# Slab loads in the forward's plan, B's Wqkv transposed between the passes, early dWo in two parts

## The chip, the cores and the metric

One Trainium2 chip, one core of it. The time is device microseconds of one execution; the kernel before has a median of 2160.57 µs over 3 runs (2158.79 to 2169.59). One more execution was profiled: it took 2162.31 µs, and its span in the profile, from the first to the last instruction, is 2160.6 µs.

## What is computed

A forward pass through four layers (A, B, A, B) and its gradients, in bf16, for S = 2048 tokens, D = 640, H = 32 heads of 20:

```python
def _A_ref(x, wqkv, wo):                       # linear attention
    q, k, v = split_heads(x @ wqkv)
    phi = lambda t: jnp.where(t > 0, t + 1, jnp.exp(t)) + 1e-6
    kv  = einsum("bhsd,bhse->bhde", phi(k), v); z = einsum("bhsd->bhd", phi(k))
    o   = einsum("bhqd,bhde->bhqe", phi(q), kv) / (einsum("bhqd,bhd->bhq", phi(q), z) + 1e-6)
    return merge_heads(o) @ wo
def _B_ref(x, wqkv, wo):                       # causal softmax attention, window of 256
    ...
x = x + _A_ref(_layernorm(x), A_wqkv, A_wo)    # layer 0
x = x + _B_ref(_layernorm(x), B_wqkv, B_wo)    # layer 1
x = x + _A_ref(_layernorm(x), A_wqkv, A_wo)    # layer 2, the same weights
x = x + _B_ref(_layernorm(x), B_wqkv, B_wo)    # layer 3, the same weights
_out, _vjp = jax.vjp(_f, A_x, A_wqkv, A_wo, B_wqkv, B_wo); _grads = _vjp(grad_out)
```

The outputs are the last x and the gradients of x and of the four weights. The gradient of B's output weight, dWo, is the sum over layers 3 and 1 of (attention output, transposed) x (gradient that arrives at the layer). For layer 3 that gradient is grad_out itself, so this half of dWo can be formed as soon as the forward has layer 3's attention outputs.

## The kernel before, in words

The program is one class. `run()` calls `forward()`, then the attention backward of layer 3 (`B_attn_bwd(3)`), a phase of matmuls and layer norms (`bwd_phase(3, 2, 1)`), the attention backward of layer 1, and the last phase (`bwd_phase(1, 0, None)`).

**Forward.** Tokens go in 16 tiles of 128. `a_first(0)` and `a_kv(0)` do layer 0 up to its key-value sums. `ab_pass(0)` runs the rest of layer 0, layer 1 and the first part of layer 2 as one pipeline over the tiles. After it `late_q(2)` gives the queries of layer 2 for the first six tiles as fillers, `a_kv(2)` sums layer 2, and `ab_pass(2, True)` runs the rest of layer 2 and layer 3. In that second pass each tile of layer 3 also has its local gradient: `dO_steps` multiplies grad_out by Wo and stores dO (with two further columns a head) to DRAM as `dOpt`. q, k and v of layer 3 are stored to DRAM as `qkvp`.

What a tile of layer 3 does on the engines: TensorE makes 12 score matmuls for a group of four heads (L794), ScalarE (ACT) takes the exponential in two instructions (L798, L801), GpSimd (POOL) masks the diagonal and the oldest block (L807, L812), TensorE multiplies by the values (L832). The output projection (`out_proj`, Wo_B), the residual addition to x, the store of the finished x (`out_dram`), and the two chunks of dO follow.

**What sets the order.** In the forward every instruction is an `op` of a planner (`Sched`): engine, an assumed cost, keys that it reads and writes. `order()` is a list scheduler: each engine takes the op that can start first by the assumed times, among equals the one that was written first; TensorE may look 19 ops ahead of the first one not yet issued. `emit()` issues everything in that order with the order fixed, so each engine's queue is exactly the plan. The written order within a pass comes from due times in units of tiles (`items`, `spread`). Buffers come from rings: a ring of n hands out its tiles in turn, and a new use waits for all users of the use n before.

DMAs are issued from SP's or ACT's queue. Each is queued behind what its engine waits for. The DMAs share eight semaphore lanes: a DMA that takes a lane waits for the one that had it before.

**The end of the forward.** After the second pass come `bflips`: 15 blocks of 128 x 640 of B's Wqkv are transposed by DMA into the rings `ee` and `pp` and stored to DRAM as `WqTB`, gated by the layer norm of tile 15 in layer 3. Then `early_dWo` (L715 to L730): 10 units (5 row blocks x 2 halves of 320 columns) of 16 matmuls each (L723; 128x128 by 128x320), in a ring of two PSUM buffers `mm`, an ACT copy each (L727), and a store from ACT's queue to `dWoB_part`.

**The attention backward.** It works on 8 groups of four heads. For each group `attn_slabs` loads slabs from DRAM: q, k, v and dO transposed (QTg, KTg, VTg, dOTg), and k, q, dO plain (Ksl, Qsl, dOsl); for group 0 the dO ones in two halves of 8 tiles. For layer 3 group 0's loads are issued on SP after the forward. For each group 15 steps follow: pairs of scores and dP on TensorE (L1583), exponential on ACT (L1602), masks on POOL (L1611, L1614), product on VectorE (L1622), a transpose of the product and the accumulating matmuls. Layer 1's group 0 is loaded ahead, within `bwd_phase(3)`, to a region `slabA`.

Of the kernel before, what the change touches and what calls it, by code (L numbers as in the profile page):

```python
# [10 lines left out]
ACT = mybir.ActivationFunctionType  # L11
# [5 lines left out]
P = 128  # L17
# [183 lines left out]
class Kern:  # L201
# [130 lines left out]
    def forward(self):  # L332
# [5 lines left out]
        with ExitStack() as st:  # L338
# [5 lines left out]
            def ring(name, n, shape, dt=BF, **kw):  # L344
# [13 lines left out]
                hnA=ring("hnA", 1, [P, D]), hnTA=ring("hnTA", 3, [P, DT, P]),  # L358
                hnB=ring("hnB", 1, [P, D]), hnTB=ring("hnTB", 3, [P, DT, P]),
# [4 lines left out]
                rt=ring("rt", 2, [P, H], F32), li=ring("li", 2, [P, H], F32),  # L364
            )
            pk = g = self.g
# [14 lines left out]
            R["res"] = Ring(2, tiles=[over_vv(CW) for _ in range(2)], name="res")  # L381
# [4 lines left out]
            wsb = {k: big.tile([P, DT, n], BF, name=k) for k, n in (("Wqkv_B", QT), ("Wo_A", D))}  # L386
# [282 lines left out]
            def b_qkv(l, tt, hnT, qk, v, qT, kT):  # L669
                qkvp_v = self.tm_view(self.sv[l]["qkvp"])  # L670

                def chunk(ci):
                    def f():
# [13 lines left out]
                        if ci in (1, 3):  # L687
# [4 lines left out]
                                [(b, ci - 1), (b, ci)], [])  # L692
                        if ci == 5:
                            dma("SP", lambda: qkvp_v[:, tt, 2 * DP:3 * DP], lambda: v.t.rearrange("p h d -> p (h d)"),
                                256 * KB, [(v, 4), (v, 5)], [])
# [20 lines left out]
            def early_dWo():  # L716
                for m in range(DT):
                    for ci in range(2):
                        ps, res, c0 = R["mm"].buf(), R["res"].buf(), ci * CW
                        for t0, t1 in ((0, 5), (5, 10), (10, TT - 1), (TT - 1, TT)):  # L720
                            def f(ps=ps, m=m, c0=c0, t0=t0, t1=t1):
                                for tt in range(t0, t1):
                                    nc.tensor.matmul(ps.t[:, 0:CW], lhsT=att_out[3, tt][0].t[:, m * P:(m + 1) * P],  # L723
                                                     rhs=g[:, tt, c0:c0 + CW], start=(tt == 0), stop=(tt == TT - 1))
                            op("PE", pe([CW] * (t1 - t0)), f, [("g", tt) for tt in range(t0, t1)] +
                               [(att_out[3, tt][0], q) for tt in range(t0, t1) for q in (0, 1)], [ps])
                        op("ACT", av(CW), lambda ps=ps, res=res: nc.scalar.copy(res.t, ps.t[:, 0:CW]), [ps], [res])  # L727
                        after_kv(S.ops[-1])
# [1101 lines left out]
```

## Time and profile before

| | |
|---|---|
| median of 3 runs | 2160.57 µs (2158.79 to 2169.59) |
| the profiled execution | 2162.31 µs, span 2160.6 µs |
| mean granted TensorE clock | 0.974 |
| PE busy 93%, DVE 66%, ACT 55%, POOL 41% of the span | |
| pass 0 ends, a_kv(2), pass 2 begins | about 398 to 480 µs |
| last score group of the forward | 722.23 µs |
| early dWo on PE | 731.85 to 753.74 µs |
| first pair of the attention backward, layer 3 | 754.52 µs |
| first pair of the attention backward, layer 1 | 1480.91 µs |

Times in rows are microseconds from the start of the span. A row in order of time gives start, length, engine, line of the kernel, operation, what it writes and reads, and how often; rows that follow one another closely are merged. In brackets stands the idle time of the engine before the row, and what ended it. SPq and ACTq are DMA issues on the queues of SP and ACT. Rows "A <- B: us, times, longest" sum what A waited for B. Matmuls are pipelined: the time from one row's start to the next is what counts, not the sum of lengths. Rows by stretch give for each engine busy time and, in brackets, instructions, then the granted TensorE clock (1 is full), the DMA engines' mean busy share, and GB/s.

### The profile page before, as it was taken

The page shows a single profiled execution, that of the slowest core. Times are in us where ns is not written, and L with a number is a line of the kernel's source. Part 1 is how long each engine was busy: PE and PEld are TensorE (multiplying, and loading weights), DVE is VectorE, ACT ScalarE, POOL GpSimd, SP SyncE. Part 2 cuts the span into 40 slices and gives each one's busy share as a digit, 9 for nine tenths or more (in the row PEclk, how much of TensorE's full clock was granted, in tenths as well). Part 3 has the DMA queues.
Part 4 walks back from the last instruction along what each step waited for, and adds up shares of the span by engine and source line. Part 5 has one row for each costly group of instructions (what it writes and reads, how often), then busy time and mean ns, then how long its engine had stood idle before and what let it go on. Part 6 is the DMA issues. An engine that isn't in the chain of part 4 may idle for free. (4 is left out here: it accounts for less than half of the span.)

```text
span 2160.6 us, 67815 instructions
## 1 busy us (share of the span) xinstructions
PE 2004.4 (93%) x27808; PEld 1383.7 (64%) x27808; DVE 1436.1 (66%) x2942; ACT 1195.3 (55%) x1981; POOL 883.0 (41%) x1850
## 2 busy tenths in 40 slices
PE   6878899879999799999899999998999999999999
PEld 4645666556666567777666667645777766666764
DVE  7667677577776289999734459705999985444751
ACT  4627778627788389989622223314989982220430
POOL 1015566416777356666422213203666652220210
PEclk9989999999999889999999999998999999999999
DMA  7459989469999799998998799936999998989944
GB/s 273 172 151 198 194 192 194 116 191 201 210 210 203 167 164 155 156 161 156 180 187 183 197 201 210 186 95 143 158 161 158 157 179 171 197 184 225 183 112 103
DMA packets 964807, 379.70 MB, mean 176 GB/s; under 512 B 844816, under 2 KB 944784, under 8 KB 964240
## 3 DMA queue, kind: packets, MB, share of 16 engines
q1 hardware_dynamic: 886720, 301.59, 72.7%
q10 hardware_dynamic: 77776, 73.79, 11.1%
q8 instruction: 217, 3.56, 0.7%
q14 instruction: 94, 0.77, 0.1%
HBM read 109.02 MB, written 112.07 MB: 102 GB/s over the span
## 5 line engine op out<-in xcount | busy, mean ns | idle before, releaser
L1622 DVE TENSOR_TENSOR ds_sb<-pair,e_sb 128x768 bf16<-128x768 f32 x480 | 438.0, 951 | 78.7 <-PE pair L1583 71.9
L1602 ACT ACTIVATE e_sb<-pair 128x768 bf16<-128x768 f32 x480 | 391.1, 815 | 92.7 <-PE pair L1583 68.0
L807 POOL TENSOR_SCALAR_AFFINE_SELECT e_sb<-e_sb 128x384 bf16<-128x384 bf16 (+1 forms) x512 | 199.5, 409 | 359.5 <-ACT e_sb L798 333.9
L798 ACT ACTIVATE e_sb<-s_ps 128x1152 bf16<-128x1152 f32 (+2 forms) x256 | 273.9, 1070 | 112.5 <-PE s_ps L794 76.9
L1614 POOL TENSOR_SCALAR_AFFINE_SELECT e_sb<-e_sb 128x256 bf16<-128x256 bf16 x448 | 183.1, 409 | 225.7 <-ACT e_sb L1602 225.6
L1068 PE MATMUL dw_ps<-dqkv,om 128*128 128x480 bf16 x1280 | 268.8, 366 | 0.0
L1068 PEld LDWEIGHTS <-om 128*128 128x128 bf16 x1760 | 170.7, 98 | 152.1 <-DMA om<-o 8.1
L1256 POOL TENSOR_TENSOR gw<-w,gcar 128x640 f32<-128x640 f32 x64 | 89.5, 1399 | 421.7 <-ACT w L1253 417.6
L1611 POOL TENSOR_SCALAR_AFFINE_SELECT e_sb<-e_sb 128x256 bf16<-128x256 bf16 x512 | 207.4, 408 | 102.0 <-ACT e_sb L1602 102.0
L1068 PEld LDWEIGHTS <-dqT 128*128 128x128 bf16 x1920 | 185.7, 98 | 71.8 <-issue 0.4
L1647 PEld LDWEIGHTS <-dsT 128*128 128x128 bf16 x2880 | 146.2, 97 | 94.9 <-issue 88.6
L1638 ACT COPY dsT<-dsT_ps 128x768 bf16<-128x768 bf16 x240 | 191.2, 797 | 9.5 <-PE dsT_ps L1635 6.3
L439 PE MATMUL mm_ps<-Wqkv_B,hnTB 128*128 128x320 bf16 x960 | 169.8, 308 | 9.6 <-DVE gcar L511 5.9
L1647 PE MATMUL dqvk_ps<-Ksl,dsT 128*128 128x32 bf16 x2160 | 170.4, 179 | 7.3 <-DMA dsT<-ds_sb 4.5
L1651 PE MATMUL dqvk_ps<-dOsl,e_sb 128*128 128x32 bf16 x2160 | 165.7, 177 | 0.1
L1651 PE MATMUL dqvk_ps<-Qsl,ds_sb 128*128 128x32 bf16 x2160 | 165.8, 177 | 0.0
L1635 PE MATMUL dsT_ps<-ident,ds_sb 128*128 128x128 bf16 x1848 | 157.9, 223 | 1.5 <-ACT dsT L1638 1.3
L1651 PEld LDWEIGHTS <-e_sb 128*128 128x128 bf16 x2880 | 144.9, 96 | 0.2 <-issue 0.2
L1651 PEld LDWEIGHTS <-ds_sb 128*128 128x128 bf16 x2880 | 145.0, 96 | 0.0
L812 POOL TENSOR_SCALAR_AFFINE_SELECT e_sb<-e_sb 128x512 bf16<-128x512 bf16 x224 | 143.1, 639 | 0.0
L801 ACT ACTIVATE e_sb<-s_ps 128x384 bf16<-128x384 f32 (+2 forms) x256 | 119.7, 468 | 36.3 <-PE s_ps L794 13.6
L1068 PE MATMUL dw_ps<-wq,dqT 128*128 128x320 bf16 x960 | 138.1, 299 | 0.3 <-ACT dqkv L1428 0.3
(209 smaller groups left out, 3900.7 us busy)
## 6 DMA issues: line engine op xcount, KB each, us to landing
qkvp<-qk_slab SPq DMA_DIRECT2D x64, 256.0 KB, 3.5
hn<-hn SPq DMA_DIRECT2D x64, 160.0 KB, 3.1
om<-hn SPq DMA_DIRECT2D x20, 512.0 KB, 5.2
qkvp<-v_slab SPq DMA_DIRECT2D x32, 256.0 KB, 3.8
o<-o SPq DMA_DIRECT2D x48, 160.0 KB, 3.1
om<-o SPq DMA_DIRECT2D x15, 512.0 KB, 4.8
Ksl<-qkvp SPq DMA_DIRECT2D x12, 512.0 KB, 5.2
Qsl<-qkvp SPq DMA_DIRECT2D x12, 512.0 KB, 5.3
```

What stands on the lines that cost most here:

```text
L439: nc.tensor.matmul(ps.t[:, w0:w0 + width], lhsT=lhsT(), rhs=rhs(), start=start, stop=stop)
L798: op("ACT", av(3 * nkt * P), lambda: nc.scalar.activation(e.t[:, 0:3, 0:nkt, :], s3.t[:, :, 0:nkt * P].rearrange("p h (i q) -> p h i q", q=P),
L807: nc.gpsimd.affine_select(out=v, in_=v, compare_op=ALU.is_ge, fill=0.0, base=0, pattern=[[0, h1 - h0], [1, P]], channel_multiplier=-1)
L1068: nc.tensor.matmul(ps.t[:, w0:w0 + width], lhsT=lhsT(), rhs=rhs(), start=start, stop=stop)
L1602: nc.scalar.activation(E[n][:, 2 * p:2 * p + 2], PR[h][:, :, 0:3 * P].rearrange("p i (j q) -> p i j q", q=P), ACT.Exp, scale=self.c_att)
L1611: nc.gpsimd.affine_select(out=e[:, :, j, :], in_=e[:, :, j, :], compare_op=ALU.is_ge, fill=0.0, base=0, pattern=[[0, 2], [-1, P]], channel ...
L1614: nc.gpsimd.affine_select(out=e[:, :, j, :], in_=e[:, :, j, :], compare_op=ALU.is_ge, fill=0.0, base=-1, pattern=[[0, 2], [1, P]], channel ...
L1622: nc.vector.tensor_mul(DS[n][:, hs], PR.pop(h)[:, :, 0:3 * P].rearrange("p i (j q) -> p i j q", q=P), E[n][:, hs])
L1635: nc.tensor.transpose(ps[:, i, j, :], DS[n][:, 2 * p + i, j, :], self.ident)
L1638: (nc.scalar.copy if by == "A" else nc.vector.tensor_copy)(TSB[h], TPS.pop(h))
L1647: nc.tensor.matmul(a[:, 0, hh, :], lhsT=TSB[2 * n + hh // 2][:, hh % 2, j, :], rhs=ld[g]["K"][:, k, cs], start=(i == 0), stop=(i == len(dq ...
L1651: nc.tensor.matmul(a[:, 1 + x, hh, :], lhsT=src[n][:, hh, j, :], rhs=ld[g][rhs][:, q, cs], start=(i == 0), stop=(i == len(dkv) - 1))
```

## The change

- A new tile `slabR` of 7 x 2048 columns lives for the whole program. It holds group 0's slabs of layer 3. During the forward, Wqkv_B, Wo_A and the small rings hnA, hnB, rt, li are cut from it; later the backward of layer 3 uses it for even groups' slabs, that of layer 1 for odd groups', and the phases cut rings and sums from it.
- Group 0's nine slab loads become ops of the forward's plan on SP. They wait for the stores that they read and for all readers of Wqkv_B and Wo_A (the plain dO loads also for the users of the small rings).
- The 15 `bflips` stand between the two passes, gated by layer 1's last layer norm, and go through the rings KT, QT and e.
- Early dWo is in two parts. `dWo_most`: units 0 to 5, tiles 0 to 12, due at 15.0 to 16.25 of the second pass, in three chunks (5, 5, 3); the sum is copied in f32 by DVE into x of tiles that are done. `dWo_rest`, at the end: units 6 to 9 with all 16 tiles (an ACT copy each), then the last three tiles of units 0 to 5, added by DVE to what lies in x. It uses the score ring's five PSUM buffers and waits for the last two scores.
- The stores of x and dO of tiles 14 and 15 are issued on SP instead of ACT.

```diff
-    def forward(self):
+    def forward(self, slabs):
...
+            wsb = {k: over_raw(DT * n).rearrange("p (k n) -> p k n", k=DT) for k, n in (("Wqkv_B", QT), ("Wo_A", D))}
+            for k in ("hnA", "hnB"):
+                R[k] = Ring(1, tiles=[over_raw(D)], name=k)
...
+            TS, NA = 13, 6
+
+            def dWo_mm(ps, u, t0, t1, a):
+                m, c0 = u // 2, u % 2 * CW
...
+            def dWo_most(u):
+                def f():
+                    ps = R["mm"].buf()
+                    for t0 in range(0, TS, 5):
+                        dWo_mm(ps, u, t0, min(t0 + 5, TS), 0)
+                    op("DVE", vp(CW), lambda: nc.vector.tensor_copy(x[:, u, :].bitcast(F32), ps.t[:, 0:CW]), [ps],
+                       [("x", u)])
+                return f
+
+            def dWo_rest():
+                scored = [o for k in ("s3", "s1") for b in R[k].items[-2:] for o in b.ops]
+                order = list(range(NA, 2 * DT)) + list(range(NA))
...
+                    b, ps = res[m], R["s"].buf()
...
+                    for t0 in ([0, 5, 10, TS] if u >= NA else [TS]):
+                        dWo_mm(ps, u, t0, min(t0 + 5, TS) if t0 < TS else TT, 0 if u >= NA else TS).deps.update(scored)
+                    if u >= NA:
+                        op("ACT", av(CW), lambda ps=ps, half=half: nc.scalar.copy(half(), ps.t[:, 0:CW]), [ps], [(b, ci)])
+                    else:
+                        op("DVE", vp(CW), lambda ps=ps, half=half, u=u: nc.vector.tensor_add(
+                            half(), ps.t[:, 0:CW], x[:, u, :].bitcast(F32)), [ps, ("x", u)], [(b, ci)])
...
-                        dma("ACT", lambda: self.tm_view(self.dOp[3])[:, tt, :], lambda: slab.t.rearrange(
-                            "p h d -> p (h d)"), 256 * KB, [(slab, i) for i in range(4)], [])
+                        dma("ACT" if tt < TT - 2 else "SP", lambda: self.tm_view(self.dOp[3])[:, tt, :], lambda: slab.t.rearrange(
+                            "p h d -> p (h d)"), 256 * KB, [(slab, i) for i in range(4)], [("dOp", tt)])
...
             def bflips(i, gate):
-                    b = R[("ee", "ee", "pp")[i % 3]].buf()
+                    kind = ("KT", "QT", "KT", "e", "e")[i % 5]
+                    b = R[kind].buf()
...
-                                dma("ACT", lambda: xout[:, tt, :], lambda: x[:, tt, :], 160 * KB, [("x", tt)], [])
+                                dma("ACT" if tt < TT - 2 else "SP", lambda: xout[:, tt, :], lambda: x[:, tt, :], 160 * KB,
+                                    [("x", tt)], [])
...
+                    spread(items, 15.0, 16.25, [dWo_most(u) for u in range(NA)])
...
             ab_pass(0, False)
+            for i in range(3 * DT):
+                bflips(i, ("rs", 1, TT - 1))()
             for tt in range(EARLY):
                 late_q(2, tt, filler=True)
...
             ab_pass(2, True)
-            for i in range(3 * DT):
-                bflips(i, ("rs", 3, 15))()
-            early_dWo()
+            over = [o for k in ("Wqkv_B", "Wo_A") for o in S.rd.get(k, ())]
+            late = [o for k in ("hnA", "hnB", "rt", "li") for b in R[k].items for o in b.ops]
+            for rows, kind, size, f in slabs:
+                keys = [("dOp", t) for t in rows] or [("qkvp", 3, t, i) for t in range(TT) for i in (1, 3, 5)]
+                op("SP", 60, f, keys, [], dma=(kind, size)).deps.update(over + late if rows and kind == "D" else over)
+            dWo_rest()
...
+        self.raw = self.persist.tile([P, 7 * self.T], BF, name="slabR")
...
+        first, slab0 = {}, Cuts(self.raw)
+        self.forward(self.attn_slabs(3, 0, slab0, first))
```

More of the change, by code (lines that the diff above doesn't have):

```diff
@@ L714, in early_dO @@
                     after_kv(S.ops[-1])
[L716 to L728, printed above, removed]
-                        dma("ACT", lambda m=m, c0=c0: self.dWoB_part[m * P:(m + 1) * P, c0:c0 + CW], lambda res=res: res.t,
-                            2 * P * CW, [res], [])
@@ L1138, in bwd_phase @@
                         ("pkT", 2, [P, DT, P], BF), ("vT", 2, [P, DT, P], BF), ("eq", 2, [P, D], BF), ("ek", 2, [P, D], BF)):
-                    R[name] = ring(name, n, shape, dt)
+                    if name != "ek" or far:
+                        R[name] = ring(name, n, shape, dt)
+                if not far:
+                    R["ek"] = Ring(2, tiles=[cuts.tile([P, D], BF, f"ek{i}") for i in range(2)], name="ek")
             if not wide:
@@ L1703, in B_attn_bwd @@
                        lambda g=g, t=t: evac(g, t), [("A", g, t, hh) for hh in range(4)])
[L1704 to L1708 removed]
+            ld[0] = first
             todo = {}
```

76 lines of the change are left out of this document (42 added, 34 removed).

## Prediction, made before the changed kernel was run

> **What bounds the kernel now.** I read the page's head first, then the busy time by stretches of 5 µs around the end of the forward pass, then the engines' rows in order of time there, then the longest waits.
>
> ```profile
> span 2160.6 us, 67815 instructions
> PE 2004.4 (93%) x27808; PEld 1383.7 (64%) x27808; DVE 1436.1 (66%) x2942; ACT 1195.3 (55%) x1981; POOL 883.0 (41%) x1850
> ```
>
> TensorE (PE) is busy for 93% of the span, so a change gains where PE idles, where its clock is low, or where it works alone while nothing that follows can start. The end of the forward has all three. Rows of the stretches (from:to, length, then PE, weight loads, DVE, ACT, POOL, the granted clock, the DMA share):
>
> ```profile
> 700.00:705.00 5.00, 4.19 (x58) 2.62 (x57) 0.49 (x1) 3.50 (x6) 3.82 (x9) 0.53 0.98 249
> 720.00:725.00 5.00, 2.39 (x60) 1.77 (x59) 0.00 (x0) 3.77 (x6) 3.67 (x9) 0.50 1.09 194
> 398.00:440.00 42.00, 33.57 (x523) 24.42 (x522) 25.29 (x71) 18.97 (x36) 12.46 (x28) 0.96 0.25 84
> ```
>
> PE's own rows there (start, length, what, and in brackets the idle time before):
>
> ```profile
> 696.79 0.35 PE L794 MATMUL s_ps<-QT,KT 32*128 32x128 bf16 x12
> ...
> 702.08 0.51 PE L794 MATMUL s_ps<-QT,KT 32*128 32x128 bf16 x12
> 702.52 2.85 PE L439 MATMUL mm_ps<-Wo_B,oTB 128*128 128x320 bf16 x10
> ...
> 705.37 1.49 PE L439 MATMUL mm_ps<-vv 128*128 128x320 bf16 x5
> 706.80 0.49 PE L794 MATMUL s_ps<-QT,KT 32*128 32x128 bf16 x12
> ...
> 712.27 0.35 PE L794 MATMUL s_ps<-QT,KT 32*128 32x128 bf16 x12
> 712.55 0.32 PE L832 MATMUL pv_ps<-v_slab,e_sb 128*128 128x32 bf16 x6
> 712.71 0.43 PE L439 MATMUL mm_ps<-Wo_B,oTB 128*128 128x320 bf16 x2
> ...
> 720.42 0.51 PE L794 MATMUL s_ps<-QT,KT 32*128 32x128 bf16 x12 [1.30 <-ACT e_sb L798]
> ...
> 722.23 0.51 PE L794 MATMUL s_ps<-QT,KT 32*128 32x128 bf16 x12 [0.87 <-ACT e_sb L798]
> ...
> 731.10 0.84 PE L439 MATMUL mm_ps<-vv 128*128 128x320 bf16 x5
> ...
> 733.61 2.06 PE L723 MATMUL mm_ps<-gcar,Wqkv_A 128*128 128x320 bf16 x14
> ...
> 735.79 2.06 PE L723 MATMUL mm_ps<-gcar,Wqkv_A 128*128 128x320 bf16 x14
> ...
> 753.17 0.57 PE L723 MATMUL mm_ps<-gcar,Wqkv_A 128*128 128x320 bf16 x3
> 754.52 0.35 PE L1583 MATMUL pair<-KTg,QTg 32*128 32x128 bf16 x8 [0.78 <-ACT vv L727]
> ```
>
> The last two tiles' 12 score groups start between 696.79 and 722.23, 11 periods in 25.44 µs. ACT's exponentials set the natural period: 720.42 to 722.23 is 1.81. Eleven of these are 19.9, so 5.5 µs are stalls. After the scores PE ends the last dO chunk at 731.94 (731.10 + 0.84) and then does all of early dWo alone until 753.74: 160 matmuls, 16 per 2.18 µs (733.61 to 735.79), 0.136 each. The two stalls and PE's idle time by what it waited for, and then the slab loads and the first work of the attention backward:
>
> ```profile
> ACT e_sb L798 <- DVE vv L754: 3.2, 1, 3.2
> ACT e_sb L798 <- DMA ee<-in_B_wqkv_dram: 3.2, 1, 3.2
> ```
> ```profile
> PE s_ps L794 <- ACT e_sb L798: 6.0, 5, 2.8
> PE pv_ps L832 <- POOL e_sb L812: 5.5, 6, 1.3
> ```
> ```profile
> 740.94 1.27 SPq L326 DMA_TRANSPOSE QTg<-qkvp  x1
> ```
> ```profile
> 758.27 1.82 DVE L1622 TENSOR_TENSOR ds_sb<-pair,e_sb 128x768 bf16<-128x768 f32 x2 [22.60 <-PE pair L1583]
> ```
>
> So the slab loads begin late, at 740.94, and VectorE's first product, from which the attention's own rhythm runs, comes at 758.27, 3.75 µs after the first pair.
>
> **The change, part by part.**
>
> *Dealing 13 tiles of six units under the scores.* 78 of the 160 dWo matmuls move ahead of the dO's end. By the planned order PE gets, between the score group at 696.79 and the last one, 20 Wo_B and 15 dO matmuls that were there before, 65 of dWo (units 0 to 4), about 100 value products and 11 score groups. At full clock: 100 wide ones x 0.136 = 13.6; scores 0.28 a group (712.27 to 712.55), 3.1; values 0.16 for six (712.55 to 712.71), some 3; one set of transposes, 0.3. Sum 20.4, against 25.44 that pass now. Period by period the work is 0.7, 1.8, 1.8, 1.9, 1.8, 1.1, 2.3, 2.0, 1.9, 1.8 and 3.3; where it is under ACT's 1.81 the period is 1.81, which makes 22.3. The stall on the DMA goes: it is ACT standing at an out_dram store that shares a semaphore lane with a Wqkv flip; the flips are moved away and the store goes to SP. Full clock is not to be had throughout: the row of 700 to 705 has 0.53, and what leads to it is not changed. Ten Wo_B took 2.85 at 702.52 where 10 x 0.136 is 1.4, and about the next 1.2 µs of work doubles as well before the busier PE is fast again; half of some 4 µs, 2.0, is added. (Bounds: 0, and 4 if it lasts to 708 as now.) The last scores then start at 696.79 + 22.3 + 2.0 = 721.1, not 722.23.
>
> After it, to the end of dO, PE has 42 value products, 10 Wo_B, 10 dO and 8 transposes as now, 13 matmuls of unit 5 and 8 + 5 of the whole units in gaps that are waits for POOL, DVE and ACT. It takes 9.7 µs now (722.23 to 731.94), at the 0.50 of 720 to 725; with more work but a warmer clock I take 9.35: 730.45. Left are 61 of dWo (units 6 to 9 less what was in the gaps, and 6 x 3): 61 x 0.136 = 8.3, PE ends at 738.7 instead of 753.74: **-15.0**. The copies to x (six, on DVE) and the six additions lie in time in which DVE idles: 0.49 busy of 5 in the first stretch, none in the second. Without that cover the last addition alone would be on the path, about 0.5.
>
> *Slab loads in the plan.* Seven of the nine need only q, k, v and the first dO tiles, all done by 703; they stand on SP from there, ahead of the last stores. The two second halves of dO follow dO's last store. What that gives is seen where layer 1 starts, with its slabs loaded ahead:
>
> ```profile
> 1480.91 0.35 PE L1583 MATMUL pair<-slabA 32*128 32x128 bf16 x8
> ```
> ```profile
> 1481.92 2.36 ACT L1602 ACTIVATE e_sb<-pair 128x768 bf16<-128x768 f32 x3 [24.36 <-DVE res L1171]
> ```
> ```profile
> 1483.61 2.69 DVE L1622 TENSOR_TENSOR ds_sb<-pair,e_sb 128x768 bf16<-128x768 f32 x3 [2.10 <-POOL e_sb L1611]
> ```
>
> 2.70 from first pair to first product, so 1.05 less than in layer 3. But there is a new wait. The last dWoB_part store on ACT shares a lane with the load of dO's second half, and the first exponential is queued on ACT behind that store. The chain of it, with the store's row now and the landing times:
>
> ```profile
> 735.46 0.34 ACTq L407 DMA_DIRECT2D dOpt<-vv  x1
> ```
> ```profile
> WqTB<-ee SPq DMA_DIRECT2D x10, 160.0 KB, 2.8
> dOpt<-vv ACTq DMA_DIRECT2D x4, 256.0 KB, 3.4
> ...
> Qsl<-qkvp SPq DMA_DIRECT2D x1, 512.0 KB, 5.3
> ...
> ee<-in_B_wqkv_dram SPq DMA_TRANSPOSE x8, 4.3
> ...
> dOTg<-dOpt SPq DMA_TRANSPOSE x2, 3.5
> ```
>
> From the dO's end to the store are 3.5 µs (731.94 to 735.46), its landing 3.4, the load's landing 3.5, the freed store's issue 0.3: 730.45 + 10.7 = 741.2. Without it the exponential would start at 738.7 + 0.8 (the pair's wait for an evacuation, as at 754.52) + 1.0 = 740.5. So the exponential is at 741.2, and the product 1.7 later (1481.92 to 1483.61), at 742.9: **-15.4** against 758.27.
>
> *Flips between the passes.* 15 flips and 15 stores on SP, and their place on it:
>
> ```profile
> 722.34 1.28 SPq L411 DMA_TRANSPOSE pp<-in_B_wqkv_dram  x1
> 723.66 0.58 SPq L407 DMA_DIRECT2D WqTB<-pp  x1
> ```
> ```profile
> 403.53 23.24 SPq L407 DMA_DIRECT2D hn<-hnA  x3
> ```
> ```profile
> 478.26 0.28 PE L439 MATMUL mm_ps<-mbd,pqT 128*128 128x32 bf16 x5
> ```
>
> 15 x (1.28 + 0.58) = 28 µs of SP. SP there issues three hn stores in 23 µs, mostly waiting, and the DMA share of 398 to 440 is 0.25, so the flips fit up to about 437. Behind them stand the pqT flips of later tiles, the third of which PE needs at 478.26. New lane sharing holds single ACT stores for about 1 µs. ACT is busy 18.97 of 42 there. I take **+1.0**, with bounds -1 and +3.
>
> *The rest.* The order of PE from the attention backward on is the old one, so a shift at 758 is carried to the end. The backward phases cut their rings from the new tile; loads wait for the same last readers to within a group, and the memsets of layer 1's sums move a little on DVE: 0, within 1.5 either way. The absence of the 15 flips from the forward's end is counted with the stall; the DMA share of about 1 there makes anything more possible, nothing less.
>
> **Sum**: -15.4 + 1.0 = -14.4. The profiled execution took 2162.31 µs (span 2160.6 and 1.7 around it), so it becomes 2147.9; it was 1.74 above the median of three, 2160.57, and by the same step the median becomes **2146.2**.
>
> **Rivals.**
>
> 1. *The clock stays high* (0.14). With dWo in the waits PE has hardly a gap, so the 0.53 stretch may vanish, and the moved flips cost nothing: 2.0 and 1.0 more gain, and 1 from DMA relief: -17.4 to -18.4, 2142 to 2143. For it: PE's waits in 690 to 760 are 6.0 for ACT and 5.5 for POOL, and those are what is filled. Against it: the drop to 0.53 comes before the first dealt matmul.
> [...]
>
> 2. *The dealt matmuls delay the scores* (0.14). PE takes its queue in order. A chunk of 5 is 0.68 at full clock and 1.36 at half; each ahead of a score group can hold ACT, which is the rhythm. 18 chunks at 0.6 are 10.6 µs, all that was moved. If nothing hides, what stays is the DMA stall (up to 3.2), the 1.05 of the slabs, and 1 to 3 of filled waits after the last scores, less 1.0: -4 to -6, so 2155 to 2157. For it: six periods are over 1.81 even at full clock. Against it: 5.5 µs of stalls and 6.0 of waits for ACT are there to be filled.
>
> 3. *The slabs do not come early* (0.12). The lane chain above is within 0.7 µs of the bound. Each of its landings at 5.3, the Qsl row, instead of 3.4 and 3.5 delays the first exponential by 3.7: 2149.9. So the change would not do in full what its first part says. For it: seven loads and four stores on one SP queue, and a DMA share near 1. Against it: the flips that fill the queues now are gone.
>
> 4. *Slower* (0.06): the flips between the passes run one at a time. Each store waits for its flip, each buffer for its store, behind scores and values that use the same buffers: 15 x (4.3 + 2.8) = 106 µs from 403.53, to 510. The pqT flip behind them would be 32 late at PE's 478.26, less 15.4: +16, 2177. It decides from (478.3 - 403.5 + 15.4) / 15 = 6.0 µs a flip. Against it: eleven buffers are in rotation, not one, and the DMA share there is 0.25, where the present place has about 1.
>
> **How the numbers follow.** The forecast has 0.54, spread over 2143 to 2150. About 0.5% (10.8 µs) is what a measurement of this kernel can tell from no change, which puts the border at 2149.8. Faster: 0.51 of the forecast's, 0.14 of the first rival and 0.06 of the third, 0.71. Same: 0.03, 0.14 and 0.06, 0.23. Slower: 0.06. The range goes from 2140 (first rival, with the memsets' 1.5) to 2156.5 (most of the second), and leaves out the fourth and some of the ends.
>
> **What would show it.** Right: dWo rows between the last score groups; PE's last dWo matmul near 739; the slab loads from about 703; the first product near 743, and the same shift up to the end; no ACT wait of 3 µs for a flip after 710; 398 to 480 longer by no more than 3. Wrong: score periods of 2.5 and more with ACT waiting for PE (second); a first exponential after 743 held by a store (third); a PE wait for pqT between 440 and 480 (fourth); clock 1.0 in 700 to 710 (first). A changed length between 760 and the end would mean that the rings' new places matter, which I cost at nothing.

## The result, and the profile after

| | before | after | ratio after / before |
|---|---|---|---|
| first comparison, median of 22 executions each | 2161.78 µs | 2156.60 µs | 0.9974 [0.9962, 0.9985] |
| a second comparison (35 and 12 executions) | 2165.67 µs | 2157.50 µs | 0.9963 [0.9950, 0.9977] |
| the profiled execution (span) | 2162.31 µs (2160.6) | 2163.08 µs (2161.4) | |

By the ratios the change gains 5.6 µs (0.26% of 2161.78; the two medians differ by 5.2) in the first and 8.0 µs in the second comparison; 14.4 were forecast. The sign was right, the size was not: 2156.60 lies just above the range's upper end, 2156.5. The profiled execution of after happens to be one of its longest, so its span can't be set against that of before; its parts can.

The page's head for after, then three stretches of the forward's end:

```profile
span 2161.4 us, 67833 instructions
PE 2008.5 (93%) x27808; PEld 1384.3 (64%) x27808; DVE 1441.9 (67%) x2954; ACT 1191.9 (55%) x1975; POOL 879.2 (41%) x1850
```
```profile
700.00:705.00 5.00, 4.01 (x67) 2.67 (x66) 3.54 (x8) 3.36 (x5) 4.43 (x8) 1.00 0.27 57
720.00:725.00 5.00, 4.21 (x77) 2.97 (x76) 1.32 (x3) 4.04 (x6) 2.92 (x7) 1.00 1.16 216
702.00:753.00 51.00, 45.59 (x649) 31.88 (x647) 24.68 (x55) 25.25 (x37) 26.66 (x54) 1.00 0.65 150
```

The clock is 1.00 in the two windows in which before had 0.53 and 0.50. As this profile stands 12 µs late here (see below), its 702 to 753 is the work that before does from 690 to 741. The clock is 1.00 over it, against 0.80:

```profile
690.00:741.00 51.00, 38.51 (x552) 26.27 (x551) 18.84 (x44) 25.25 (x36) 27.16 (x55) 0.80 0.78 162
```

PE's rows of after at the forward's end, then ACT's and DVE's first work of the attention backward:

```profile
732.36 0.34 PE L828 MATMUL s_ps<-QT,KT 32*128 32x128 bf16 x12
...
740.63 0.84 PE L446 MATMUL mm_ps<-vv 128*128 128x320 bf16 x5
741.31 0.98 PE L730 MATMUL s_ps<-gcar,Wqkv_A 128*128 128x320 bf16 x6
...
749.87 1.38 PE L730 MATMUL s_ps<-gcar,Wqkv_A 128*128 128x320 bf16 x9 [0.65 <-DVE hnTA L761]
751.18 0.57 PE L1629 MATMUL pair<-slabR 32*128 32x128 bf16 x8
753.73 1.20 PE L1629 MATMUL pair<-slabR 32*128 32x128 bf16 x10 [1.98 <-ACT e_sb L1648]
```
```profile
752.87 1.51 ACT L1648 ACTIVATE e_sb<-pair 128x768 bf16<-128x768 f32 x2 [4.42 <-DMA dWoB_part<-pp]
```
```profile
754.55 2.71 DVE L1668 TENSOR_TENSOR ds_sb<-pair,e_sb 128x768 bf16<-128x768 f32 x3 [2.13 <-PE pair L1629]
```

This profile of after stands 12.1 µs late when the last two tiles' scores begin: the group that started at 696.79 in before starts at 708.90. With 12.1 taken off, the forecast's steps read:

| step | forecast | after, less 12.1 |
|---|---|---|
| last score group | 721.1 | 720.3 |
| end of dO on PE | 730.45 | 729.4 (740.63 + 0.84) |
| end of dWo on PE | 738.7 | 739.1 (749.87 + 1.38) |
| first exponential | 741.2 | 740.8 |
| first product | 742.9 | 742.4 |

The forecast of this stage held to about 1 µs, the first exponential by some luck. As named, it stands on ACT behind the last dWoB_part store. But that store did not wait for its lane. These are SP's dO store and the load of dO's second half, DVE's last additions, and the stores:

```profile
744.98 0.33 SPq L414 DMA_DIRECT2D dOpt<-vv  x1
747.07 1.17 SPq L326 DMA_TRANSPOSE slabR<-dOpt  x1
```
```profile
750.47 1.69 DVE L761 TENSOR_TENSOR pp<-s_ps,x 128x320 bf16<-128x320 f32 x4 [0.66 <-PE s_ps L730]
```
```profile
751.00 1.77 ACTq L414 DMA_DIRECT2D dWoB_part<-pp  x4
```

The dO store landed in 2.0 µs and the load in 3.1, where 3.4 and 3.5 were assumed, so the lane was free at 750.2. The last store went out at 752.4, behind the last addition, which ends at 752.2. The forecast's two paths to the exponential, by the lane and by PE, lay 0.7 apart, so the time came out although the path was the other one.

So 15.5 µs were won here, and 12.1 were missing before it began.

To see where, the start of each PE matmul in before is subtracted from its start in another kernel's profile. A step of this shift is time that one section lost or won. A single profile wanders: the kernel before, profiled once more, was 3.3 late at 420 and 4.5 at 1812 with nothing changed. So each section is read over all profiles:

| kernel | between the passes, 403 to 520 | end of forward, 692 to 763 | 1779 to 1800 | another section | sum | measured, from the ratio |
|---|---|---|---|---|---|---|
| after | +6.4 | -15.5 | +4.0 | | -5.1 | -5.6 |
| after again | +7.2 | -15.6 | +2.6 | | -5.8 | -8.0 |
| before again | +3.3 | -1.1 | +0.9 | | +3.1 | +1.5 |
| flips only | +6.3 | -2.9 | +1.4 | | +4.8 | +0.9 |
| flips after hn | +12.7 | -15.7 | +3.6 | | +0.6 | +2.4 |
| dWo at the end | +6.2 | -5.9 | +3.1 | | +3.4 | +7.8 |
| flips first | -0.4 | -15.7 | +1.8 | +14.0 before 150 | -0.3 | +3.7 |
| memset last | +6.1 | -15.4 | +0.9 | | -8.4 | -7.1 |
| flips first, memset last | -0.5 | -15.8 | +2.5 | +14.2 before 150 | +0.4 | -1.5 |
| flips in pass 2 | +4.2 (to about 480) | -15.8 | +2.7 | +31.1 (480 to 692) | +22.2 | +19.9 |
| flips at the end | +1.6 | -2.7 | +2.8 | | +1.7 | +2.8 |
| slabs in the program | +7.3 | -15.5 | +3.7 | | -4.5 | -7.4 |
| small flips | +7.7 | -15.8 | +2.7 | +13.3 before 113 | +7.9 | +6.3 |

The sum is that of the columns ahead of it, without the drift in the sections that no kernel changes. The last column is (ratio - 1) times the median of before on that chip. Sum and measurement differ by up to 4.4 (dWo at the end), which is how far a single profile can be trusted.

### The profile page after: what moved, and what is told of

The parts are those of the page before. It is cut to its first block, busy times and chain, and to the rows that moved or that the text cites. A ratio compares the mean times of both kernels' runs of the same rounds, so it can differ in the third digit from the quotient of the medians.

```text
span 2161.4 us, 67833 instructions
## 1 busy us (share of the span) xinstructions
PE 2008.5 (93%) x27808; PEld 1384.3 (64%) x27808; DVE 1441.9 (67%) x2954; ACT 1191.9 (55%) x1975; POOL 879.2 (41%) x1850
## 3 DMA queue, kind: packets, MB, share of 16 engines
q10 hardware_dynamic: 77200, 72.94, 10.9%
## 5 line engine op out<-in xcount | busy, mean ns | idle before, releaser
L1113 PEld LDWEIGHTS <-slabR 128*128 128x128 bf16 x1920 | 185.7, 98 | 116.2 <-DMA slabR<-o 5.8
L446 PE MATMUL mm_ps<-slabR,hnTB 128*128 128x320 bf16 x960 | 170.5, 309 | 8.4 <-DVE gcar L518 6.1
L1697 PEld LDWEIGHTS <-e_sb 128*128 128x128 bf16 x2880 | 145.2, 96 | 0.0
L1113 PE MATMUL dw_ps<-dqkv,slabR 128*128 128x480 bf16 x640 | 134.6, 366 | 0.0
L1113 PE MATMUL dw_ps<-dqkv,om 128*128 128x480 bf16 x640 | 134.2, 366 | 0.0
L1284 ACT ACTIVATE dh<-mm_ps 128x320 f32<-128x320 f32 x64 | 28.0, 437 | 191.6 <-PE mm_ps L1113 153.3
L1629 PE MATMUL pair<-slabR 32*128 32x384 bf16 (+2 forms) x1024 | 121.6, 329 | 11.5 <-DVE ds_sb L1668 5.0
L866 PE MATMUL pv_ps<-v_slab,e_sb 128*128 128x32 bf16 x2880 | 117.7, 177 | 12.9 <-POOL e_sb L846 10.7
L866 PEld LDWEIGHTS <-e_sb 128*128 128x128 bf16 x2880 | 106.0, 96 | 35.6 <-POOL e_sb L846 14.6
```

What stands on the lines that cost most here:

```text
L446: nc.tensor.matmul(ps.t[:, w0:w0 + width], lhsT=lhsT(), rhs=rhs(), start=start, stop=stop)
L866: nc.tensor.matmul(pv.t[:, h % 16, :], lhsT=e.t[:, hh, j, :], rhs=vts[j].t[:, h, :], start=(j == 0), stop=(j == nkt - 1))
L1113: nc.tensor.matmul(ps.t[:, w0:w0 + width], lhsT=lhsT(), rhs=rhs(), start=start, stop=stop)
L1697: nc.tensor.matmul(a[:, 1 + x, hh, :], lhsT=src[n][:, hh, j, :], rhs=ld[g][rhs][:, q, cs], start=(i == 0), stop=(i == len(dkv) - 1))
```

## The experiments

Each was timed in five rounds (flips small in three) against the kernel before on the same chip.

**The kernel before, once more.** No edit. Expected:

> The kernel before with nothing changed, as a second look at it. In the two profiles at hand the changed kernel is 6 us late already at 440 us, in a part of the forward that the change does not reorder. If that is chance between two executions, this profile differs from the first one of the kernel before by several us there too (up to 6), and its time ratio is 1.000 within 0.1%. Rival: cutting the small rings and two weights from the new tile costs 6 us early in the forward; then this profile agrees with the first one within 1 us at 440, and every kernel with the new tile is some 6 late there.

Measured: 1.0007 [0.9991, 1.0022]. So intervals of this width can tell 0.2 to 0.3%, and the +5.4 that after's first profile shows at 300 µs, where nothing was changed, is most likely chance: before again is at +3.0 there, and the other kernels in which the first 300 µs of work are those of after are at -2.6 to +4.5.

**The flips alone** (before, with the 15 flips between the passes and through the rings KT, QT and e):

```diff
             ab_pass(0, False)
+            for i in range(3 * DT):
+                bflips(i, ("rs", 1, TT - 1))()
...
             ab_pass(2, True)
-            for i in range(3 * DT):
-                bflips(i, ("rs", 3, 15))()
             early_dWo()
```

> The kernel before with one part of the change alone: the 15 flips of Wqkv between the passes. Theory (queue): the store of hn of the last tile stands on SP behind flips that wait for buffers; an ACT store shares its lane, ACT stands some 6 us, PE idles 3 and falls to half clock: pass 2 starts about 6 us later (from 420 to 490), and the end of the forward wins back 3 (no ACT wait for a flip): ratio about 1.0015. Rival (my forecast): +1 there, so -2 in all: 0.999.

Measured: 1.0004 [0.9988, 1.0019]. The transition is 6.3 longer, the forward's end 2.9 shorter. Alone, the move gains nothing that can be measured.

The waits between the passes show where ACT stands. In before, in after, and with the flips alone (5.4 to 5.8 µs for a store of hn, which is issued on SP among the flips):

```profile
ACT ee L507 <- DMA pk<-gcar: 2.6, 1, 2.6
```
```profile
ACT ee L514 <- DMA hn<-slabR: 5.8, 1, 5.8
ACT ee L514 <- DMA linv<-slabR: 5.1, 1, 5.1
PE mm_ps L446 <- DVE gcar L518: 3.4, 1, 3.4
```
```profile
ACT ee L507 <- DMA hn<-hnA: 5.4, 1, 5.4
```

SP's rows in after around that store, then PE's matmuls behind it, and the same matmuls in before:

```profile
431.60 1.72 SPq L418 DMA_TRANSPOSE e_sb<-in_B_wqkv_dram  x1
433.37 1.27 SPq L418 DMA_TRANSPOSE KT<-in_B_wqkv_dram  x1
434.69 1.28 SPq L418 DMA_TRANSPOSE QT<-in_B_wqkv_dram  x1
436.08 0.52 SPq L414 DMA_DIRECT2D hn<-slabR  x1
```
```profile
440.96 2.83 PE L446 MATMUL mm_ps<-Wqkv_A,pqT 128*128 128x320 bf16 x10 [3.36 <-DVE gcar L518]
```
```profile
432.02 1.52 PE L439 MATMUL mm_ps<-Wqkv_A,pqT 128*128 128x320 bf16 x10 [0.19 <-DVE gcar L511]
```

An hn store of layer 2 is issued behind flips at 436.08 and lands 3.1 µs later, at 439.2. ACT's store of v is on the same lane and goes out at 439.27, and ACT stands idle from 433.86 to 439.67. The evacuations behind it come late, PE idles 3.36 µs, and its next ten matmuls take 2.83 instead of 1.52. That is a chain of the kind that the forecast had seen at the forward's end and had taken for gone. (The 5.1 that the profile puts down to linv is not such a wait: none of the stores issued in it waited for a lane for more than 0.4 µs.)

**The hn store first.** If the chain is one store behind flips, then ordering the flips behind the hn store of tile 15 should cure it:

```diff
+                if l == 2 and tt == TT - 1:
+                    self.last_hn = S.ops[-1]
...
                 bflips(i, ("rs", 1, TT - 1))()
+                if i >= 3:
+                    S.ops[-2].deps.add(self.last_hn)
```

> The changed kernel with all flips but the first three planned behind the last tile's hn store. Theory (queue): the ACT wait for that store goes from 5.8 to under 2, PE is not idle there, and the shift between 420 and 490 falls from 6 to 2 or less; against the kernel before the ratio goes from 0.9974 to about 0.9955. Rival (bandwidth): the transfers between the passes cost because the DMA engines are fuller (0.86 for 0.51), in whatever order; the shift stays at 5 to 7 and the ratio at 0.997.

Measured: 1.0011 [0.9997, 1.0025], a transition of +12.7. A miss: ACT's wait for the hn store is gone, but the flips now stand later, and other stores of ACT wait for them: eq and pq go out at 441.62 and 442.22, right behind the landing of a WqTB store (441.54) and of a flip (442.15) on their lanes. A wait of 9.9 for DVE's statistics follows (5.5 in after), whose cause was not followed:

```profile
ACT rs L477 <- DVE mv L476: 12.6, 3, 9.9
...
ACT ee L557 <- DMA e_sb<-in_B_wqkv_dram: 4.1, 1, 4.1
```

**All of dWo at the end** (`TS, NA = 13, 0`: no unit under the scores).

> The changed kernel with all ten dWo units whole at the end, none among the scores. If the matmuls among the scores are what the end of the forward gains (78 x 0.136 = 10.6 us, less what the PE waits after the last scores can take), its end gain falls from 16.5 to 6 to 8 us, PE's last dWo matmul stands 8 to 10 us later, and the ratio to before is 1.001 to 1.0025. Rival: the gain at the end comes from the removed stalls, the clock and the early slabs; then the gain falls by under 4 and the ratio is at most 0.9995.

Measured: 1.0036 [1.0020, 1.0051]. Between the passes it loses the same 6.2; at the end it wins 5.9 instead of 15.6. So dealing the matmuls is worth 9.7 µs in the profiles and is the largest part of the gain. By the ratios it is 0.62% (1.0036 against 0.9974) to 0.73% (against after again), 13 to 16 µs; the 4 to 6 µs between the two readings are not explained.

**The changed kernel, once more** (no edit), beside the next three:

> The changed kernel again, beside the next three on the same chip: ratio to the kernel before 0.9974 within 0.0015. In its profile, against the first one of the kernel before: 15 to 16.5 us won between the last scores' stretch and the attention backward (690 to 775), 5 to 7 lost between 416 and 490, and 3 to 4 lost between 1790 and 1812. What differs by more than 2 from the first profile of the changed kernel is chance.

Measured: 0.9963 [0.9950, 0.9977].

**Flips during layer 0's first pass**, one for each tile:

```diff
+            for i in range(3 * DT):
+                items.append((i + 1.85, len(items), bflips(i, ("rs", 0, i + 1))))
             run(items)
...
-            for i in range(3 * DT):
-                bflips(i, ("rs", 1, TT - 1))()
```

> The changed kernel with the 15 flips dealt one a tile over layer 0's first pass (10 to 60 us), where their eleven buffers are unused and the DMA share is 0.5 to 0.6. If what costs is their place between the passes, the loss between 416 and 490 falls from 6 to at most 2.5 (what the kernel before shows between its own two profiles), layer 0's pass loses at most 2, and the ratio to before goes from 0.9974 to 0.9945 to 0.996. Rival: 30 more DMAs cost some 5 us wherever ACT and SP have stores in flight (lanes and landing times): then the loss moves to the first 113 us and the ratio stays at 0.997.

Measured: 1.0017 [0.9998, 1.0035]. The transition is back at -0.4, so the 6 µs do go with the flips. But 14 µs are lost where the flips now are. PE gets 118 matmuls done in 40 to 60 µs instead of 160 (before, then this kernel):

```profile
40.00:60.00 20.00, 17.56 (x160) 12.99 (x159) 15.94 (x46) 12.91 (x31) 0.00 (x0) 1.00 0.47 166
```
```profile
40.00:60.00 20.00, 15.30 (x118) 10.63 (x117) 10.77 (x30) 8.90 (x22) 0.00 (x0) 0.89 0.63 182
```

**The large memset last.** In layer 1's last phase a region of 128 x 1920 that must be zero is cut from `slabR` in after. In the rows of before and after it has changed sides of the attention's last evacuations:

```profile
1796.68 1.73 DVE L1144 MEMSET sums<- 128x1920 uint32 x2 [0.35 <-issue]
```
```profile
1789.63 1.66 DVE L1190 MEMSET slabR<- 128x1920 uint32 x1 [0.35 <-issue]
```

DVE does it ahead of an evacuation, and PE waits for that: 1.20 µs at the next row of after, where its other waits for these are 0.50:

```profile
1791.61 0.24 PE L1693 MATMUL dqvk_ps<-slabR,dsT 128*128 128x32 bf16 x3 [1.20 <-DVE dqkv L1707]
...
1793.23 0.24 PE L1693 MATMUL dqvk_ps<-slabR,dsT 128*128 128x32 bf16 x3 [0.50 <-DVE dqkv L1707]
```

The edit cuts the region from slabs that are read later:

```diff
-                mbdT, dmbd, dmbdT = part(DT + 1, D), part(DT, NX), part(DT + 1, D)
+                mbdT, dmbdT, dmbd = part(DT + 1, D), part(DT + 1, D), part(DT, NX)
```

> The changed kernel with the last phase's largest cleared region cut from where group 7's slabs are read last, so that DVE clears it after the attention's evictions and not between them. If the memset among the evictions is what costs 2.5 us more than before at the end of layer 1's attention, the loss between 1790 and 1812 falls from 3 to 4 to about 1, and the ratio goes down by 0.001. Rival: that loss is chance, or follows from something else (the loads from the new tile); then it stays at 3 to 4.

Measured: 0.9967 [0.9949, 0.9985], the same as after within the intervals, which can't tell 0.1%. The profile can. The memset starts at nearly the same time as in after, but this profile stands 4.9 µs earlier there, so it has moved: one evacuation is left behind it, where after has four. PE's waits at this place are 0.50, without the 1.20:

```profile
1789.30 1.66 DVE L1190 MEMSET slabR<- 128x1920 uint32 x1 [1.12 <-PE dqvk_ps L1697]
1790.88 0.34 DVE L1707 TENSOR_TENSOR dqkv<-dqvk_ps,ckv 128x240 bf16<-128x240 f32 x1
```
```profile
1786.88 0.23 PE L1693 MATMUL dqvk_ps<-slabR,dsT 128*128 128x32 bf16 x3 [0.50 <-DVE dqkv L1707]
```

From the matmul that before starts at 1790.02 to the last matmul of the attention, before, before again, flips alone and the two kernels with this edit take 4.9 µs, the nine others 6.3 to 6.4. So the memset among the evacuations costs 1.4 to 1.5. The section as a whole, 1779 to 1800, costs 3.0 on average in these nine and 0.8 in before, before again and flips alone. What is left of the difference is the clock in the matmuls behind, which differs from profile to profile: 30 of them take 4.24 here (granted clock 1.00 in 1788.7 to 1793.0) and 5.91 with both edits (0.71 in 1791.0 to 1796.9).

```profile
1788.73 4.24 PE L1113 MATMUL mm_ps<-wq,dqT 128*128 128x320 bf16 x30
```
```profile
1791.02 5.91 PE L1113 MATMUL mm_ps<-wq,dqT 128*128 128x320 bf16 x30
```

**Both of the last two edits.**

> Both of the edits before it. If both losses are what the queue theory and the memset theory say, the ratio to before is 0.993 to 0.995, all of the gain of the end (15 us, 0.7%). Rival: they are chance or move elsewhere; 0.997.

Measured: 0.9993 [0.9976, 1.0010]: the 14 µs in layer 0 again, and the memset's 1.5 gone again.

**Flips dealt over the second pass** (through the ring hnTA, gated by layer 3's norms).

```diff
+                    for i in range(3 * DT):
+                        items.append((0.8 * i + 0.55, len(items), bflips(i, ("rs", 3, int(0.8 * i)))))
...
-            for i in range(3 * DT):
-                bflips(i, ("rs", 1, TT - 1))()
```

> The changed kernel with the 15 flips dealt over pass 2 (one in 0.8 tiles, through the ring hnTA), where TensorE is 96% busy and ACT has a quarter of its time free. What has been seen: between the passes the flips cost 6 us, in layer 0's first pass 13, both times through stores that share lanes or a ring of one buffer with them. If the cost is in what waits behind a store there, the loss between 416 and 490 falls to 2.5 or less, pass 2 (490 to 690) gets at most 3 longer, and the ratio to before is 0.994 to 0.996. Rival: 30 more DMAs at a DMA share of 0.96 lengthen pass 2 by more than the 6 won: 0.997 to 1.001.

Measured: 1.0092 [1.0069, 1.0115]. 31 µs are lost in 480 to 692. The planner also orders PE otherwise with them, so this is the price of the place and of the new order together. For the 13 µs in layer 0's first pass the path through lanes and a ring is the expectation's reading: with the flips there, ACT's waits put down to a DMA are 3.3 µs for pq and 1.5 for eq in 40 to 124, where before has 1.8 for ek; how the rest was lost is not shown.

**Flips at the end** as in before, but through the rings of after, with all else changed.

> The changed kernel with the flips back at the end of the forward, ahead of the slab loads. If the forward's end gains by the flips being away (the ACT wait of 3.2, and a free SP for the slabs), its gain between 690 and 775 falls from 15.5 to 9 to 12, and the slab loads begin later; the loss between 416 and 490 falls to at most 2.5: together 0.996 to 0.998, about as the changed kernel. Rival: the end does not need them away; then the gain stays at 15 and the ratio is 0.994 to 0.995.

Measured: 1.0013 [0.9998, 1.0029]. The transition is nearly clean (+1.6), and of the end's gain 2.7 is left. The rows of the waits at the end:

```profile
ACT e_sb L1648 <- DMA WqTB<-e_sb: 17.4, 1, 17.4
...
PE pair L1629 <- ACT e_sb L1648: 15.0, 1, 15.0
```

PE is done with dWo early, and then the first exponential starts 17.4 µs after ACT's work before it. That wait has two parts, by ACT's rows:

```profile
741.69 3.27 ACTq L414 DMA_DIRECT2D dWoB_part<-pp  x4
753.63 1.51 ACT L1648 ACTIVATE e_sb<-pair 128x768 bf16<-128x768 f32 x2 [17.45 <-DMA WqTB<-e_sb]
```

ACT's last store is out at 744.96. For the other 8.7 µs the exponential itself waits, until the store WqTB<-e_sb of a flip, issued at 750.33, has landed at 753.52. The exponential's row is an ACTIVATE, not a DMA issue, so it takes no lane itself. It writes a buffer e_sb, and the flips of this kernel go through the ring e; that its buffer lies where that store still reads is argued from these names, not shown. Without this part the end would have gained up to 2.7 + 8.7 = 11.4 (an estimate from these rows), within what was expected. So of the 13 µs that the flips at the end take from the gain, up to 8.7 may be the price of the buffers that they went through, and the run does not show what they would cost there in the rings `ee` and `pp` of before. Away they save 2.9 at the end by themselves (flips alone).

**Slab loads in the program after the forward** instead of in its plan.

```diff
-                op("SP", 60, f, keys, [], dma=(kind, size)).deps.update(over + late if rows and kind == "D" else over)
+                pass
...
+        early = self.attn_slabs(3, 0, slab0, first)
+        self.forward(early)
+        with self.tc.manual_schedule(engines={mybir.EngineType.SP}):
+            for _, _, _, f in early:
+                f()
```

> The changed kernel with group 0's slab loads issued after the forward's plan, as before. If the early slabs are worth what layer 1's start shows (1.05 us) and what the loads themselves take beyond dWo's shorter tail (the nine loads took 18 us from the first issue to the last in the kernel before, and dWo's tail behind the last scores is now some 19 less what they wait for), the gain at the end falls from 15.5 by 1 to 8, and the ratio to before is 0.997 to 1.000. Rival: the loads fit behind the tail anyway; then the gain falls by less than 1.

Measured: 0.9966 [0.9952, 0.9979]. It did not undo what it meant to: the loads still stand among the last tiles' work,

```profile
708.83 2.28 SPq L326 DMA_TRANSPOSE slabR<-qkvp  x1
```

so it counts as another repeat of the changed kernel and says nothing of the slabs' share.

**Flips with a fifth of the bytes**, in the same places with the same 30 DMAs:

```diff
-                    flip(view, lambda: self.B_wqkv[et * P:(et + 1) * P, part * D:(part + 1) * D], 160 * KB, [gate], [b])
+                    flip(view, lambda: self.B_wqkv[et * P:(et + 1) * P, part * D:part * D + P], 160 * KB, [gate], [b])
...
+            dma("ACT", lambda: W["WqTB"].rearrange("p (k n) -> p k n", k=DT), lambda: self.B_wqkv.rearrange("(k p) n -> p k n", p=P), 0, ["masks"], [])
```

> The changed kernel with each flip and its store cut to one block of five (128 x 128 for 128 x 640): the same 30 DMAs in the same places of SP's queue, on the same lanes and buffers, with a fifth of the bytes. WqTB is filled at the start by one plain copy of the untransposed weight, so two weight gradients and what follows from them are not the reference's, and the start is longer by what that copy takes. Theory (traffic): what costs between the passes is that the flips' bytes double the landing times of the stores there (1.8 to 3.2 us), on which ACT waits lane by lane; then the loss between 416 and 490 falls from 6 to at most 2.5 and the landing times are back at 1.8 to 2.2. Theory (places): what costs is the number of DMAs in SP's queue and on the lanes; then the loss stays at 4 to 6.

Measured: 1.0029 [1.0014, 1.0044], of which 13.3 µs are the added copy at the start. Two theories stood: the flips' traffic slows the other transfers, or their places in queue and lanes hold up stores. The stretch 395 to 480 of before, after and this kernel, then landing times of after and this kernel in 416 to 456:

```profile
395.00:480.00 85.00, 68.11 (x864) 47.29 (x863) 56.27 (x148) 30.21 (x66) 19.32 (x44) 0.96 0.51 147
```
```profile
395.00:480.00 85.00, 64.65 (x862) 45.17 (x850) 51.33 (x135) 29.93 (x56) 18.64 (x42) 0.94 0.86 200
```
```profile
395.00:480.00 85.00, 64.65 (x933) 45.59 (x925) 51.31 (x134) 35.83 (x66) 24.27 (x54) 0.96 0.52 138
```
```profile
v<-vv ACTq DMA_DIRECT2D x3, 160.0 KB, 3.7
```
```profile
v<-vv ACTq DMA_DIRECT2D x4, 160.0 KB, 1.9
```

The DMA share falls back from 0.86 to 0.52 and the landing of v from 3.7 to 1.9, yet the transition loses 7.7, and ACT waits for a flip itself:

```profile
ACT ee L514 <- DMA e_sb<-in_B_wqkv_dram: 5.2, 1, 5.2
```

The theory of the traffic falls. What is left are the DMAs' places: SP's order, the lanes shared with ACT's stores, and the buffers. For ACT's standing still the traces decide among them, as they tell the lane and the landing of every DMA. In the waits of 5.8 (after), 5.4 (flips alone) and 5.2 (this kernel) ACT issues its stores ek, pk and v, and eight of the nine go out right behind the landing of the DMA of SP that had their lane:

| kernel | store of ACT | goes out at | the DMA of SP before it on its lane | issued | landed |
|---|---|---|---|---|---|
| after | ek | 434.30 | flip into e_sb | 429.60 | 434.22 |
| after | pk | 435.65 | flip into e_sb | 431.60 | 435.58 |
| after | v | 439.27 | hn | 436.08 | 439.19 |
| flips alone | pk | 428.25 | flip into e_sb | 424.26 | 428.16 |
| flips alone | v | 432.44 | hn | 429.50 | 432.37 |
| flips small | ek | 444.37 | flip into QT | 441.96 | 444.29 |
| flips small | pk | 445.53 | WqTB store | 443.87 | 445.45 |
| flips small | v | 448.40 | flip into e_sb | 446.12 | 448.32 |

So it is the lanes that hold ACT (these eight go out 0.07 to 0.09 µs after the landing), and SP's order that makes the DMAs on them late. Summed over the work that before does from 403 to 470, ACT waited for lanes held by DMAs of SP:

| kernels | ACT's wait, µs | loss of the section |
|---|---|---|
| the five without flips there (before, before again, flips first, both edits, flips at the end) | 1.5 to 1.8 | -0.5 to +3.3 |
| the six with them (after, after again, flips alone, dWo at the end, memset last, slabs in the program) | 5.1 to 6.7 | +6.1 to +7.3 |
| flips small | 8.8 | +7.7 |
| flips after hn | 10.9 | +12.7 |

The wait rises with the loss. No run changes the lanes alone, so the share of the loss that goes with them is read from these waits and not tested by itself.

## Why the prediction was wrong

**Right: the end of the forward** (-15.4), with a path and a count that were not. The nine profiles with the flips away and 13 tiles dealt give -15.6 on average, before and before again -0.6, so about -15.1. The times under it were right too (table above), with two compensations. 2.0 µs were charged for a clock at half, which did not come (1.00 over 702 to 753), and the rest of the stage took a little longer. Of the 4 µs at half behind that charge, the row at 702.52 of before shows 2.85; the next 1.2, and a busier PE being fast again after them, were the author's estimate, which no run shows. Before itself has 0.50 in 700.33 to 707.15, with PE busy for 6.01 of these 6.82 µs. And the first exponential came on time by PE's path and the last stores, not by the lane that was named as the last to come free. Two sums of the working are off without weight: the terms of the 20.4 add up to 20.0, and its places for the 160 dWo matmuls hold 152 (65, 13, 13 and 61); PE's rows of after do have 61 behind the dO's end.

**Wrong: the step "flips between the passes", +1.0 with bounds -1 and +3.** It cost 5.8: +6.6 on average in the six profiles that have the flips there with free gates (after, after again, flips only, dWo at the end, memset last, slabs in the program), +0.8 in the five that don't. The step added up SP's issue time and found that it fits, which it does. It costed "new lane sharing" at about 1 µs of single ACT stores, an estimate of the author's that no run shows. The traces show 3.3 to 5.2 µs more of it in the six profiles (5.1 to 6.7 against 1.5 to 1.8), most of it in one stand of ACT, where each store is held until a DMA that was issued late on SP has landed (tables under the last experiment). The price is the other queue's backlog, not one landing. The forecast had the row for it: at the forward's end of before, a store that shared a lane with a flip had held ACT for 3.2 µs.

**Too narrow: "the rest", 0 within 1.5.** The section 1779 to 1800 costs 2.2 more with `slabR` (3.0 against 0.8). The memset among the last evacuations is 1.4 to 1.5 of it, and both runs that moved it won that back; the rest goes with the clock in the matmuls behind (30 of them in 4.24 µs at 1.00 and in 5.91 at 0.71, above).

Together: -15.1 + 5.8 + 2.2 = -7.1, between the two measurements of -5.6 and -8.0.

**The rivals.** The first one's clock was right, 1.00 over 702 to 753, but not its conclusion: the gain at the end came out as without it, and the moved flips cost more, not nothing. In these profiles the clock goes with the dealt matmuls: over the stretches of 5 µs from 690 to 725 its lowest is 0.50, 0.68, 0.64 and 0.77 in the profiles without them (before, before again, flips alone, dWo at the end) and 1.00 in those with them (after, after again, flips at the end). By what rule it falls is not shown: in before the 0.53 came behind waits of at most 1.0 µs for POOL (690 to 702). The second did not happen, though PE did keep to its queue (in before it idles 2.79 µs for ACT ahead of the scores at 718.61, with all of dWo behind them): the last score group came 0.8 earlier than forecast. The third neither: the first product came at 742.4. The fourth named the right place and the wrong wait: PE waits not for pqT behind 15 serial flips, 32 late, but for an evacuation behind a held store, 3.2 late (3.36 against 0.19), with 1.3 more in slower matmuls (2.83 against 1.52, at a granted clock of 0.50 in 439.65 to 446.48).

## What to carry to other kernels

A DMA that is moved to a stretch with idle queues and a low DMA share is not thereby free: here 15 flips and their stores, moved to where the share was 0.51 (395 to 480), cost 5.8 µs. Ask which stores of other queues share a semaphore lane with it, and charge the whole time until it has landed, its own queue ahead of it included, to whatever is queued behind those stores. Fitting work into waits near the end pays in full only when nothing else holds the next stage's first instruction: with the flips at the end, the landing of a flip's store held it for 8.7 µs. Where a gain of 15 µs is forecast and 6 are seen, compare starts of the same instruction section by section, over several profiles of both kernels, because one profile wanders by itself: before again was 4.5 µs late at 1812 with nothing changed, and after 5.4 at 300. For the same reason a row has moved or not by its place among its neighbours, not by its time.

## What the runs showed of the hardware

- The flips cost no less with a fifth of their bytes: the landing of the store of v fell from 3.7 to 1.9 µs, and the loss stayed (7.7 against 6.4).
- The clock dip of before (0.53 in 700 to 705) came in both of its profiles: the second has 0.81, 0.85 and 0.68 in three of the four stretches of 5 µs from 705 to 725, after's second profile 1.00 in all four. PE's waits there are short, at most 1.0 µs for POOL and 0.8 for ACT in 695 to 715 of that second profile; PE was busy for 3.4 to 4.0 of each 5 µs in 700 to 715. In the first profile the clock is 1.00 in 696.92 to 700.33, where PE is busy for 1.41 µs, 0.50 in 700.33 to 707.15, where it is busy for 6.01, and 1.00 again up to 717.39.
- No DMA went out on a semaphore lane before the one that had it had landed, also where another queue had issued that one: in before and in after alike, SP and ACT issue 1727 DMAs on eight lanes, and of the 1719 that follow another on their lane (577 and 589 of them one of the other queue) none goes out less than 0.016 µs after its landing. Eight stores on ACT's queue went out 0.07 to 0.09 µs after a DMA of SP's queue had landed (tables under the last experiment).
